# Reassociated matrix products in a four-layer linear-attention and GLU kernel, forward and backward

## The chip, the cores and the metric

The kernel runs on one core of a Trainium2 chip, as one program with one launch. The metric is device time in microseconds (us) from start to end of an execution. The engines are TensorE (PE, with its weight loads PEld), VectorE (DVE), ScalarE (ACT), GpSimd (POOL) and SyncE (SP, which issues DMAs). Each engine takes its instructions from its own queue, in order.

## The reference

Four residual layers share two sets of weights: A (linear attention), B (gated linear unit), A, B. The kernel returns the result and the gradients for the input and for the five weights. Sequence 2048, width 512, 32 heads of 16, inner width 1376, bf16.

```python
def _A_ref(x, wqkv, wo):
    qkv = (x @ wqkv).reshape(B, S, 3, H, Dh).transpose(2, 0, 3, 1, 4)
    q, k, v = qkv[0], qkv[1], qkv[2]
    phi = lambda t: jnp.where(t > 0, t + 1, jnp.exp(t)) + 1e-6
    pq, pk = phi(q), phi(k)
    kv = jnp.einsum("bhsd,bhse->bhde", pk, v)
    z = jnp.einsum("bhsd->bhd", pk)
    num = jnp.einsum("bhqd,bhde->bhqe", pq, kv)
    den = jnp.einsum("bhqd,bhd->bhq", pq, z)[..., None] + 1e-6
    o = num / den
    return o.transpose(0, 2, 1, 3).reshape(B, S, D) @ wo

def _B_ref(x, w_gate, w_up, w_down):
    g = jnp.einsum("bsd,df->bsf", x, w_gate)
    u = jnp.einsum("bsd,df->bsf", x, w_up)
    return jnp.einsum("bsf,fd->bsd", _sigmoid(g) * u, w_down)

x = A_x
x = x + _A_ref(_layernorm(x), A_wqkv, A_wo)
x = x + _B_ref(_layernorm(x), w_gate, w_up, w_down)
x = x + _A_ref(_layernorm(x), A_wqkv, A_wo)
x = x + _B_ref(_layernorm(x), w_gate, w_up, w_down)
# outputs: x, and the gradients for grad_out of A_x, wqkv, wo, w_gate, w_up, w_down
```

## The kernel before, in words

The sequence is cut into 16 row tiles of 128 rows (`st`), the width into 4 chunks of 128 (`NDC`). The residual rows stay in SBUF in float32 (`k.xs`, names `x_93` to `x_108`) and hold the running gradient later. Activations that backward needs go to DRAM in bf16 (`sv_...`). The tile framework orders the instructions of all engines when the program is built: what is written one after another in the code can be interleaved in the queues, so that the matmuls of a weight-gradient stage (`..._p2`) stand between those of a loop that waits for other engines. SP issues nearly all DMAs; only the last stage (names `ta_...`) uses ACT's queue for loads.

`a_fwd` (layers 0 and 2) runs in three stages. For each tile it projects q, k and v (L468, 12 matmuls of 512 columns), forms pq and pk with exp, min and max (L472 to L478), copies v, and transposes pq. Then z = sum of pk (L498, one column each) and kv = pk^T v (L504) over all tiles, masked to the heads' diagonal blocks (`rhsN`). Then, for each tile, num (L521), den (L524), the reciprocal (L528), o = num / den (L530), its transposes, y = o wo (L542), and the add to the residual on POOL (L546). The layer norm of a tile (`FwdLN`) gives h and its transpose hT; the one of the next layer is begun for two tiles (`NPRE`). In both `a_fwd` calls the weights' transposes for backward (`wT_groups`, 52 in all) are interleaved from the fifth tile on.

`b_fwd` (layers 1 and 3) computes the gate, the up product, the transposes and the down product tile by tile.

`a_bwd_p1` has two loops over the tiles. Loop 1: gT (cast on POOL L676, transposes), do = g wo^T (L958), its product with o and the sum over a head (L961, L963), dnA (L966, L968), dkv accumulated over tiles (L973), dnT (L979, L980), dpq (L933, L935), dq (L938) and its transposes. Between the loops the small kv gradients are masked and transposed. Loop 2: transposes of pk and v (L1028), dpk (L1055, L1057), dv (L1061), the transposes of dk and dv, dh = [dq dk dv] wqkv^T (L1038, 12 matmuls), and the layer norm's backward (`ln_bwd_tile`, L646 to L652). `a_bwd_p2` gives the weight gradients from saved rows: dwo = o^T g (L885) and dwqkv = h^T [dq dk dv] (L833). Layer 2's results are kept in DRAM (`dwp_...`), and the later layer's are added to them (L838, `final`).

The order of the backward is b_bwd_p1(3), a_bwd_p1(2), b_bwd_p2(3), b_bwd_p1(1), a_bwd_p2(2), a_bwd_p1(0), b_bwd_p2(1), a_bwd_p2(0).

Of the kernel before, what the change touches and what calls it, by code (L numbers as in the profile page):

```python
# [8 lines left out]
BF16 = mybir.dt.bfloat16  # L9
F32 = mybir.dt.float32  # L10
# [40 lines left out]
def kernel(  # L51
# [18 lines left out]
    phases = "all"  # L70
# [6 lines left out]
    k.phases = phases  # L77
# [44 lines left out]
    for l in range(4):  # L122
# [3 lines left out]
        if l % 2 == 0:  # L126
            for nm in ("pq", "pk", "v", "o"):
                d[nm] = dram.tile([S, D], BF16, name=f"sv_{nm}{l}")
            d["dqkv"] = dram.tile([S, 3 * D], BF16, name=f"sv_dqkv{l}")
# [12 lines left out]
        wqkv=dram.tile([D, 3 * D], BF16, name="dwp_wqkv"),  # L142
        wo=dram.tile([D, D], BF16, name="dwp_wo"),
# [8 lines left out]
    with tc.tile_pool(name="wfwd", bufs=1) as wfwd:  # L152
# [17 lines left out]
        with ExitStack() as lctx:  # L170
# [6 lines left out]
            lns = [FwdLN(k, l) for l in range(4)]  # L177
            if phases != "fwd":
                wtg = wT_groups(k)
                half = 26  # L180
                with tc.tile_pool(name="wt_stage", bufs=2) as wt_stage:
                    a_fwd(k, 0, lns[0], nxt=lns[1],
                          extra=lambda ps_pool: [g(wt_stage, ps_pool) for g in wtg[:half]])
                b_fwd(k, 1, lns[1], nxt=lns[2])
                with tc.tile_pool(name="wt_stage2", bufs=2) as wt_stage:
                    a_fwd(k, 2, lns[2], nxt=lns[3],
                          extra=lambda ps_pool: [g(wt_stage, ps_pool) for g in wtg[half:]])
            else:
                a_fwd(k, 0, lns[0], nxt=lns[1])
                b_fwd(k, 1, lns[1], nxt=lns[2])  # L190
                a_fwd(k, 2, lns[2], nxt=lns[3])
# [9 lines left out]
            b_fwd(k, 3, lns[3], out_cb=out_cb)  # L201

    if phases == "fwd":
        return
# [4 lines left out]
    with ExitStack() as bctx:  # L209
# [13 lines left out]
        def load_a_weights():  # L223
            k.woT = wb.tile([P, NDC, D], BF16, name="woT", tag="w_b")
            nc.sync.dma_start(out=k.woT[:], in_=k.wT["woT"].rearrange("(c p) j -> p c j", p=P))
            k.wqkvT = wb.tile([P, 3 * NDC, D], BF16, name="wqkvT", tag="w_a")
            nc.sync.dma_start(out=k.wqkvT[:], in_=k.wT["wqkvT"].rearrange("(c p) j -> p c j", p=P))
        k.load_b_weights, k.load_a_weights = load_b_weights, load_a_weights
# [7 lines left out]
        o1stg = bctx.enter_context(tc.tile_pool(name="out1_stg", bufs=2))  # L236
        o1cur = {}
# [872 lines left out]
```

## Time and profile before

| | |
|---|---|
| median of 3 runs (lowest, highest) | 1394.34 us (1394.27, 1397.73) |
| span of the profiled execution | 1393.1 us |
| instructions | 25045, of which 9956 matmuls |
| bytes moved by DMA | 269.77 MB, 194 GB/s on the mean |

The times are of whole executions; the profile is one execution, and its span is what its rows add up to. The median is 1.2 us above that span. In a row of the timeline the first number is the start in us from the span's start, the second the length; matmuls are pipelined, so a matmul's length (about 380 ns at 512 columns) is longer than the distance to the next one's start, which is what it costs. The stages in the trace: A-forward of layer 0 from 19.7 to 114.8 us, B-forward 1 to 254.6, A-forward 2 to 346.7, B-forward 3 to 484, b_bwd_p1(3) to 643, loops 1 and 2 of a_bwd_p1(2) to 707 and 787, the rest of b_bwd_p2(3) to 878, b_bwd_p1(1) to 1038, loops 1 and 2 of a_bwd_p1(0) to 1138 and 1217, and the last weight gradients to the end.

### The profile page before, as it was taken

To read this page: it belongs to the slowest core of one execution; us is meant where nothing else is said; L and a number is where in the kernel's file an instruction comes from. 1 tells how busy PE (TensorE), PEld (TensorE's weight loads), DVE (VectorE), ACT (ScalarE), POOL (GpSimd) and SP (SyncE) were. 2 spreads that over 40 slices of the span, in tenths; PEclk is the share of its full clock that TensorE was granted. 3 is DMA by queue.
4 is the path that set the end of the run, shared out by engine and by line. 5 is a ranking of instruction groups with operands and counts; after the bars stand their busy time and mean duration, and the time that the engine had idled before them with its cause. 6 is when DMAs were issued, how large, how long until landed. Compare 5 with 4: busy or idle time off the path is not lost. (4 is left out here: it accounts for less than half of the span.)

```text
span 1393.1 us, 25045 instructions
## 1 busy us (share of the span) xinstructions
PE 1297.9 (93%) x9956; PEld 790.1 (57%) x9956; DVE 679.9 (49%) x1468; ACT 647.3 (46%) x1168; POOL 250.5 (18%) x413
## 2 busy tenths in 40 slices
PE   4989899998899898998999999999999999988988
PEld 2555455556455444554665677555548675556767
DVE  6664644567533355665857400456640676611111
ACT  5857576775776544443547411444431447600000
POOL 4026654105633300002100100010010101100000
PEclk9999999999999999999999999999999999999999
DMA  7622334452543497547774586964568956499745
GB/s 273 230 103 103 149 152 158 147 177 98 201 178 143 169 326 259 175 168 237 218 230 148 181 227 149 334 217 167 172 199 248 275 169 192 143 311 261 175 122 162
DMA packets 268853, 269.77 MB, mean 194 GB/s; under 512 B 24576, under 2 KB 245184, under 8 KB 268736
## 3 DMA queue, kind: packets, MB, share of 16 engines
q1 hardware_dynamic: 246272, 253.50, 57.2%
q10 hardware_dynamic: 22464, 14.68, 3.6%
q8 instruction: 78, 1.28, 0.4%
q14 instruction: 39, 0.32, 0.1%
HBM read 144.57 MB, written 123.57 MB: 192 GB/s over the span
## 5 line engine op out<-in xcount | busy, mean ns | idle before, releaser
L730 ACT COPY ddT<-T_ps 128x1024 bf16<-128x1024 bf16 (+1 forms) x96 | 83.1, 867 | 103.4 <-PE T_ps L728 103.3
L630 POOL TENSOR_TENSOR ssd_t<-hh_t,oms 128x512 bf16<-128x512 bf16 (+1 forms) x96 | 100.6, 1052 | 83.0 <-ACT oms L628 48.4
L648 DVE SCALAR_TENSOR_TENSOR junk<-t_sb,h_ld 128x512 bf16<-128x512 f32 x64 | 46.1, 720 | 137.6 <-ACT t_sb L646 136.6
L762 DVE TENSOR_TENSOR dd_t<-dhh_ps,ssd_ld 128x512 bf16<-128x512 f32 (+1 forms) x96 | 60.4, 629 | 102.0 <-PE dhh_ps L760 102.0
L742 PEld LDWEIGHTS <-ddT 128*128 128x128 bf16 (+1 forms) x704 | 66.3, 98 | 71.4 <-issue 12.5
L468 PE MATMUL mm_ps<-wqkv,hT 128*128 128x512 bf16 x384 | 100.2, 386 | 0.5 <-DVE x_108 L601 0.4
L742 PE MATMUL dh_ps<-wuT,ddT 128*128 128x512 bf16 (+1 forms) x352 | 96.5, 382 | 3.9 <-ACT t_sb L646 0.9
L833 PE MATMUL p_ps<-p_set,p_a_15354 128*128 128x256 bf16 (+1 forms) x768 | 82.5, 267 | 10.8 <-DVE dw_stg L798 10.8
L629 DVE TENSOR_TENSOR hh_t<-u_ps,ssd_t 128x512 bf16<-128x512 f32 (+1 forms) x96 | 60.7, 634 | 65.3 <-PE u_ps L624 50.3
L760 PE MATMUL dhh_ps<-wdT,gT 128*128 128x512 bf16 (+1 forms) x384 | 87.8, 364 | 5.0 <-DMA wdT<-wdT_d 4.3
L624 PE MATMUL u_ps<-wu,hT 128*128 128x512 bf16 (+1 forms) x384 | 92.4, 361 | 0.0
L621 PE MATMUL g_ps<-wg,hT 128*128 128x512 bf16 (+1 forms) x384 | 92.0, 361 | 0.4 <-DVE ostage L530 0.4
L833 PE MATMUL p_ps<-p_set,p_a_10151 128*128 128x256 bf16 (+1 forms) x768 | 81.5, 261 | 0.9 <-DMA p_set<-sv_hdd_130 0.9
L599 PE MATMUL y_ps<-wd,hhT 128*128 128x512 bf16 (+1 forms) x352 | 81.4, 380 | 0.0
L742 PE MATMUL dh_ps<-wgT,ddT 128*128 128x512 bf16 (+1 forms) x352 | 81.3, 379 | 0.0
L833 PEld LDWEIGHTS <-p_a_15354 128*128 128x128 bf16 x768 | 68.9, 100 | 21.7 <-issue 8.4
L590 ACT COPY hhT<-hhT_ps 128x512 bf16<-128x512 bf16 (+1 forms) x96 | 49.5, 515 | 58.3 <-PE hhT_ps L587 58.1
L728 PEld LDWEIGHTS <-dd_t 128*128 128x128 bf16 (+1 forms) x704 | 50.7, 101 | 40.8 <-DVE dd_t L762 18.5
L833 PEld LDWEIGHTS <-p_a_10151 128*128 128x128 bf16 x768 | 67.2, 98 | 9.2
L728 PE MATMUL T_ps<-ident,dd_t 128*128 128x128 bf16 (+1 forms) x704 | 66.4, 221 | 3.6 <-DVE dd_t L762 3.5
L838 DVE TENSOR_TENSOR dw_stg<-p_ps,dw_stg 128x512 bf16<-128x512 f32 (+1 forms) x36 | 23.4, 653 | 87.5 <-PE p_ps L833 74.4
L1038 PE MATMUL dh_ps<-wqkvT,dkvT 128*128 128x512 bf16 x256 | 65.6, 380 | 0.0
(493 smaller groups left out, 2498.3 us busy)
## 6 DMA issues: line engine op xcount, KB each, us to landing
p_set<-sv_hdd_130 SPq DMA_DIRECT2D x15, 1024.0 KB, 7.1
p_set<-sv_hdd_119 SPq DMA_DIRECT2D x15, 1024.0 KB, 6.3
sv_ssd_118<-ssd_t SPq DMA_DIRECT2D x16, 688.0 KB, 3.1
sv_ssd_129<-ssd_t SPq DMA_DIRECT2D x16, 688.0 KB, 3.1
ssd_ld<-sv_ssd_129 SPq DMA_DIRECT2D x16, 688.0 KB, 5.5
sv_hdd_130<-dd_t SPq DMA_DIRECT2D x16, 688.0 KB, 3.9
ssd_ld<-sv_ssd_118 SPq DMA_DIRECT2D x16, 688.0 KB, 6.0
sv_hdd_119<-dd_t SPq DMA_DIRECT2D x16, 688.0 KB, 3.7
```

The lines of the kernel that those rows point to most:

```text
L468: nc.tensor.matmul(ps[:], lhsT=hT[:, kc, :], rhs=k.wqkv[:, kc, n * D:(n + 1) * D], start=(kc == 0), stop=(kc == NDC - 1))
L599: nc.tensor.matmul(y_ps[:], lhsT=T["hhT"][0:r, fc, :], rhs=k.wd[0:r, fc, :], start=(fc == 0), stop=(fc == NFC - 1))
L621: nc.tensor.matmul(g_ps[:, 0:w], lhsT=hT[:, kc, :], rhs=k.wg[:, kc, c0:c0 + w], start=(kc == 0), stop=(kc == NDC - 1))
L624: nc.tensor.matmul(u_ps[:, 0:w], lhsT=hT[:, kc, :], rhs=k.wu[:, kc, c0:c0 + w], start=(kc == 0), stop=(kc == NDC - 1))
L629: nc.vector.tensor_tensor(hh_t[:, c0:c0 + w], u_ps[:, 0:w], ssd_t[:, 0, c0:c0 + w], ALU.mult)
L630: nc.gpsimd.tensor_tensor(ssd_t[:, 1, c0:c0 + w], hh_t[:, c0:c0 + w], oms[:, 0:w], ALU.mult)
L728: nc.tensor.transpose(tps[0:r, a, i, :], dd[:, a, fc * P:fc * P + r], k.ident[:])
L730: nc.scalar.copy(ddT[:, :, fcs[0]:fcs[0] + nfull, :], tps[:, :, 0:nfull, :])
L742: nc.tensor.matmul(dh_ps[:], lhsT=T["ddT"][0:r, a, fc, :], rhs=wT[0:r, fc, :], start=(i == 0), stop=(i == n_mm - 1))
L760: nc.tensor.matmul(dhh_ps[:, 0:w], lhsT=gT[:, jc, :], rhs=k.wdT[:, jc, c0:c0 + w], start=(jc == 0), stop=(jc == NDC - 1))
L833: nc.tensor.matmul(psv[:, icl, :], lhsT=lhs_all[:, st, ic * P:(ic + 1) * P], rhs=set_t[:, st, 0:W], start=(st == 0), stop=(st == NST - 1))
L1038: nc.tensor.matmul(dh_ps[:], lhsT=lhsT, rhs=k.wqkvT[:, n * NDC + c, :], start=(i == 0), stop=(i == 3 * NDC - 1))
```

## The change

Let h be the normed rows, Wv the last third of wqkv, and g the gradient of y. Heads are blocks on the diagonal of a 512x512 matrix, which `bdmask` keeps.

Forward: X = h^T pk is accumulated during the K phase, kv = mask(Wv^T X), M = kv wo, and y = pqn M, where pqn = pq / den, row by row. v and o are never formed. den is the sum over a head of pq z, with z spread over all partitions (`zb`, by a matrix of ones). So `a_fwd` has a K phase (k projection and X), a short chain, and a Q phase (q projection, den, pqn, its transposes; y comes four tiles later, `LA`). The product pq z is on POOL.

Backward, loop 1: dp = g M^T (`MT`, computed forward), c = -sum over a head of dp pqn, and dq = (dp + c z) phi'(q) / den on VectorE and POOL, where phq - EPS, saved forward, is phi'. dz is accumulated (4 matmuls of 8 columns). G = g^T pqn comes behind the loop, kept transposed (`GT`). Then dkv = wo G masked, Nv = Wv dkv and Mv. Loop 2: dpk = h Nv plus dz, dk, and dh = dq Wq^T + pk Mv + dk Wk^T. The gradients of wo and of Wv come at the end from small matrices (`a_small_grads`): kv^T G and X dkv of both layers in one sum.

Moved besides: all 16 tiles' h and hT of an A layer are kept in SBUF (`FwdLNAll`) and hT is saved; layer 2's layer norm is done within `b_fwd` of layer 1; the weights' transposes are now in `b_fwd` 1 (w_gate, w_up, w_down: 34 groups) and `b_fwd` 3 (wqkv, wo: 16 groups). In tiles of loop 1 the loaded phq buffer is overwritten with dq and stored.

```diff
+            for nm in ("hT", "pqn", "phq", "pk"):
                 d[nm] = dram.tile([S, D], BF16, name=f"sv_{nm}{l}")
-            d["dqkv"] = dram.tile([S, 3 * D], BF16, name=f"sv_dqkv{l}")
+            d["dqk"] = dram.tile([S, 2 * D], BF16, name=f"sv_dqk{l}")
...
+            lns = [FwdLNAll(k, l) if l % 2 == 0 else FwdLN(k, l) for l in range(4)]
+            wtg_b, wtg_a = wT_groups(k)
+            a_fwd(k, 0, lns[0], nxt=lns[1])
+            with tc.tile_pool(name="wt_stage", bufs=2) as wt_stage:
+                b_fwd(k, 1, lns[1], nxt=lns[2], extra=wtg_b, wt_stage=wt_stage)
+            a_fwd(k, 2, lns[2], nxt=lns[3])
...
+            woT_GT = wb.tile([P, 2, NDC, D], BF16, name="woT_GT", tag="w_b")
+            k.woT, k.GT = woT_GT[:, 0, :, :], woT_GT[:, 1, :, :]
...
+            MT_X = wb.tile([P, 2, NDC, D], BF16, name="MT_X", tag="w_c")
+            k.MT, k.X_ld = MT_X[:, 0, :, :], MT_X[:, 1, :, :]
+            nc.sync.dma_start(out=k.MT, in_=k.sv[l]["MT"].rearrange("(c p) j -> p c j", p=P))
+            nc.sync.dma_start(out=k.X_ld, in_=k.sv[l]["X"].rearrange("(c p) j -> p c j", p=P))
...
+        a_small_grads(k, RT.big, R.stage, RT.psum)
+        a_bwd_p2(k, RT, 0, True)
...
+                (groups_a if w_sb is k.wqkv or w_sb is k.wo else groups).append(g)
...
+        h_t = self.h_all[:, st, :]
+        layernorm_tile(k, R["small"], k.xs[st], h_t, k.rstd[l][:, st:st + 1])
+        transpose_blocks(k, R["ps"], self.hT_all[:, st, :, :], [h_t[:, c * P:(c + 1) * P] for c in range(NDC)],
...
+LA = 4
...
+        def proj(st, n):
+            ps = ps_kq.tile([P, D], F32, name="mm_ps")
+            for kc in range(NDC):
+                nc.tensor.matmul(ps[:], lhsT=ln.hT_all[:, st, kc, :], rhs=k.wqkv[:, kc, n * D:(n + 1) * D],
+                                 start=(kc == 0), stop=(kc == NDC - 1))
+            return ps
...
+        def phi(ps, a_out, out):
+            e_t = work.tile([P, D], BF16, name="e_t")
+            nc.scalar.activation(e_t[:], ps[:], ACT.Exp)
+            nc.vector.tensor_scalar(a_out, e_t[:], 1.0, EPS, ALU.min, ALU.add)
+            nc.vector.scalar_tensor_tensor(out, ps[:], 1.0 + EPS, a_out, ALU.add, ALU.max)
...
+            def accum_X(st):
+                for ic in range(NDC):
+                    nc.tensor.matmul(X_ps[ic][:], lhsT=ln.h_all[:, st, ic * P:(ic + 1) * P], rhs=pk_all[:, st, :],
+                                     start=(st == 0), stop=(st == NST - 1))
...
+                ps = proj(st, 1)
+                a_t = work.tile([P, D], BF16, name="a_t")
+                phi(ps, a_t[:], pk_all[:, st, :])
...
+        z_ps = ps_kq.tile([P, D], F32, name="mm_ps")
+        for st in range(NST):
+            nc.tensor.matmul(z_ps[:], lhsT=k.ones_sq[:], rhs=pk_all[:, st, :], start=(st == 0), stop=(st == NST - 1))
+        nc.scalar.copy(zb[:], z_ps[:])
...
+            kv_ps = ps_ch.tile([P, NDC, P], F32, name="ch_ps")
             for c in range(NDC):
-                for st in range(NST):
-                    nc.tensor.matmul(z_ps[:, c:c + 1], lhsT=pk_all[:, st, c * P:(c + 1) * P], rhs=k.ones_col[:],
-                                     start=(st == 0), stop=(st == NST - 1))
-            nc.vector.tensor_copy(zcol[:], z_ps[:])
+                cs = slice(c * P, (c + 1) * P)
+                for ic in range(NDC):
+                    nc.tensor.matmul(kv_ps[:, c, :], lhsT=k.wqkv[:, ic, 2 * D + c * P:2 * D + (c + 1) * P],
+                                     rhs=X_sb[:, ic, cs], start=(ic == 0), stop=(ic == NDC - 1))
+            nc.vector.tensor_tensor(kvbdT[:], kv_ps[:], k.bdmask[:].unsqueeze(1).to_broadcast([P, NDC, P]), ALU.mult)
...
+                m_ps = ps_y.tile([P, D], F32, name="y_ps")
+                nc.tensor.matmul(m_ps[:], lhsT=kvbdT[:, c, :], rhs=k.wo[:, c, :], start=True, stop=True)
...
+                ps = proj(st, 0)
+                pq_t = work.tile([P, D], BF16, name="pq_t")
+                phi(ps, cur["phq"][:, st % NB, :], pq_t[:])
+                prod = work.tile([P, D], BF16, name="prod")
+                nc.gpsimd.tensor_tensor(prod[:], pq_t[:], zb[:], ALU.mult)
+                den = small.tile([P, H], F32, name="den")
+                nc.vector.tensor_reduce(den[:], prod[:].rearrange("p (h e) -> p h e", h=H), AX.X, ALU.add)
+                nc.vector.tensor_scalar(den[:], den[:], EPS, None, ALU.add)
+                nc.vector.reciprocal(rden_all[:, st, :], den[:])
+                pqn = cur["pqn"][:, st % NB, :]
+                nc.vector.tensor_tensor(pqn.rearrange("p (h e) -> p h e", h=H),
+                                        pq_t[:].rearrange("p (h e) -> p h e", h=H),
                                         rden_all[:, st, :].unsqueeze(2).to_broadcast([P, H, DH]), ALU.mult)
+                pqnT = stg.tile([P, NDC, P], BF16, name="pqnT", bufs=LA + 1)
...
+            def stage_y(st, pqnT):
                 y_ps = ps_y.tile([P, D], F32, name="y_ps")
                 for c in range(NDC):
-                    nc.tensor.matmul(y_ps[:], lhsT=oT[:, c, :], rhs=k.wo[:, c, :],
+                    nc.tensor.matmul(y_ps[:], lhsT=pqnT[:, c, :], rhs=M_sb[:, c, :],
...
+            Ts = {}
+            for st in range(NST + LA):
+                if st < NST:
+                    Ts[st] = stage_q(st)
+                if st >= LA:
+                    stage_y(st - LA, Ts.pop(st - LA))
...
+                    nc.tensor.matmul(m_ps[:, c * P:(c + 1) * P], lhsT=k.wo[:, c, jc * P:(jc + 1) * P],
+                                     rhs=kvbdT[:, c, :], start=True, stop=True)
...
+            if nxt is not None:
                 nxt.stage(st)
...
+            upto = (st + 1) * len(extra) // NST
+            for g in extra[done:upto]:
+                g(wt_stage, ps_tp2)
+            done = upto
...
+    h_all = p2_load_all(k, R, sv["h"], R.pfx + "_a1")
...
+            for b in range(NST // NB):
+                nc.sync.dma_start(out=pqn_all[:, b * NB:(b + 1) * NB, :], in_=dram_batch(sv["pqn"], b))
+            phld = BatchLoader(k, stg, sv["phq"], "phq_ld", nb=NB2)
...
+                nc.gpsimd.tensor_scalar(g_bf, k.xs[st][:], 1.0, 0.0, ALU.mult, ALU.add)
...
+                ph_st = phld.get(st)
+                pqn_st = pqn_all[:, st, :]
+                dp_ps = ps_mm.tile([P, D], F32, name="dp_ps")
+                for jc in range(NDC):
+                    nc.tensor.matmul(dp_ps[:], lhsT=gT[:, jc, :], rhs=k.MT[:, jc, :],
+                                     start=(jc == 0), stop=(jc == NDC - 1))
+                dp = work.tile([P, D], BF16, name="dp")
+                nc.scalar.copy(dp[:], dp_ps[:])
+                prod = work.tile([P, D], BF16, name="prod", bufs=1)
+                nc.vector.tensor_tensor(prod[:], dp[:], pqn_st, ALU.mult)
+                cneg = small.tile([P, H], F32, name="cneg")
+                nc.vector.tensor_reduce(cneg[:], prod[:].rearrange("p (h e) -> p h e", h=H), AX.X, ALU.add,
+                                        negate=True)
+                cneg_bf = small.tile([P, H], BF16, name="cneg_bf")
...
+                nc.gpsimd.tensor_copy(cneg_bf[:], cneg[:])
...
+                    nc.tensor.matmul(dz_ps[:, c, :], lhsT=pqn_st[:, c * P:(c + 1) * P],
...
+                nc.gpsimd.tensor_tensor(t_t[:].rearrange("p (h e) -> p h e", h=H),
+                                        zb[:].rearrange("p (h e) -> p h e", h=H),
+                                        cneg[:].unsqueeze(2).to_broadcast([P, H, DH]), ALU.mult)
+                nc.vector.scalar_tensor_tensor(ph_st.rearrange("p (h e) -> p h e", h=H),
+                                               ph_st.rearrange("p (h e) -> p h e", h=H), -EPS,
+                                               rden_all[:, st, :].unsqueeze(2).to_broadcast([P, H, DH]),
+                                               ALU.add, ALU.mult)
+                nc.vector.tensor_tensor(t_t[:], dp[:], t_t[:], ALU.add)
+                nc.vector.tensor_tensor(ph_st, t_t[:], ph_st, ALU.mult)
...
+            for jc in range(NDC):
+                ps = ps_mm.tile([P, D], F32, name="dp_ps")
+                for st in range(NST):
+                    nc.tensor.matmul(ps[:], lhsT=g_all[:, st, jc * P:(jc + 1) * P], rhs=pqn_all[:, st, :],
...
+                    nc.tensor.matmul(dkv_ps[:, c, :], lhsT=k.woT[:, jc, cs], rhs=GT[:, jc, cs],
...
+                    nc.tensor.matmul(ps[:, c * P:(c + 1) * P],
+                                     lhsT=k.wqkvT[:, 2 * NDC + c, ic * P:(ic + 1) * P], rhs=dkvbdT[:, c, :],
...
+                nc.tensor.matmul(ps[:], lhsT=dkvbdT[:, c, :], rhs=k.wqkvT[:, 2 * NDC + c, :], start=True, stop=True)
...
+                ops = [(T["pdT"][:, 1, c, :], k.wqkvT[:, c, :]) for c in range(NDC)]
+                ops += [(T["pdT"][:, 0, c, :], Mv[:, c, :]) for c in range(NDC)]
+                ops += [(T["dkT"][:, c, :], k.wqkvT[:, NDC + c, :]) for c in range(NDC)]
...
+                dq_st = dqld.get(st)
+                hT_st = hTld.get(st)
...
+                for a, src in enumerate((pk_st, dq_st)):
+                    for c in range(NDC):
+                        nc.tensor.transpose(tps[:, a, c, :], src[:, c * P:(c + 1) * P], k.ident[:])
+                nc.scalar.copy(pdT[:], tps[:])
...
+                    nc.tensor.matmul(dpk_ps[:], lhsT=hT_st[:, c * P:(c + 1) * P], rhs=Nv[:, c, :],
...
+            a_small_transposes(k, l, big, GT, X_ld, dkvbdT, ps_fin)
...
+def a_small_transposes(k, l, pool, GT, X_ld, dkvbdT, ps_fin):
+    nc = k.nc
+    kvbdT = k.kv[l]["kvbdT"]
+    T = {nm: pool.tile([P, NDC, w], BF16, name=nm) for nm, w in SMALL}
+    jobs = [(T["G"][:, c, :], [GT[:, i, c * P:(c + 1) * P] for i in range(NDC)]) for c in range(NDC)]
+    jobs += [(T["XT"][:, c, :], [X_ld[:, i, c * P:(c + 1) * P] for i in range(NDC)]) for c in range(NDC)]
+    jobs += [(T["kvbd"][:].rearrange("p c f -> p (c f)"), [kvbdT[:, c, :] for c in range(NDC)]),
+             (T["dkvbd"][:].rearrange("p c f -> p (c f)"), [dkvbdT[:, c, :] for c in range(NDC)])]
...
+def a_small_grads(k, pool, stg, psum):
+    nc = k.nc
+    T = {}
+    for l in (2, 0):
+        for nm, w in SMALL:
+            T[nm, l] = pool.tile([P, NDC, w], BF16, name=f"{nm}_ld{l}")
+            nc.sync.dma_start(out=T[nm, l][:], in_=k.sv[l][nm].rearrange("(c p) j -> p c j", p=P))
...
+        for i, l in enumerate((2, 0)):
+            nc.tensor.matmul(ps[:], lhsT=T["kvbd", l][:, c, :], rhs=T["G", l][:, c, :], start=(i == 0), stop=(i == 1))
...
+            for i, l in enumerate((2, 0)):
+                nc.tensor.matmul(ps[:, c * P:(c + 1) * P], lhsT=T["XT", l][:, c, ic * P:(ic + 1) * P],
+                                 rhs=T["dkvbd", l][:, c, :], start=(i == 0), stop=(i == 1))
```

## The prediction

> **What bounds the kernel now.** I read the totals first, then the stretches of the trace by stage, then single instructions. The totals and the groups give the engine:
>
> ```profile
> PE 1297.9 (93%) x9956; PEld 790.1 (57%) x9956; DVE 679.9 (49%) x1468; ACT 647.3 (46%) x1168; POOL 250.5 (18%) x413
> PE 9%; DMA 2%; DVE 0%; SPq 0%; issue 0%; DVEq 0%
> ```
>
> TensorE is busy 93% of the span. The chain that ended last covers only a tenth, so I judge by stage. The stretches of the trace (columns: length, then busy us of PE, PEld, DVE, ACT, POOL, granted clock, DMA share, GB/s) for A-forward of layer 0 (projections; kv and z; then o and y), B-forward of layer 1 and loop 1 of A-backward of layer 2:
>
> ```profile
> 19.70:79.00 59.30, 58.80 (x414) 30.89 (x412) 39.04 (x89) 49.10 (x88) 4.16 (x11) 1.00 0.62 211
> 79.00:88.20 9.20, 7.52 (x134) 7.09 (x134) 4.29 (x16) 1.17 (x2) 0.00 (x0) 0.81 0.51 173
> 88.20:114.80 26.60, 23.69 (x253) 15.02 (x253) 20.06 (x60) 16.32 (x29) 17.14 (x18) 1.00 0.20 67
> 114.80:254.60 139.80, 133.48 (x835) 70.18 (x833) 72.15 (x166) 92.13 (x189) 76.72 (x109) 0.99 0.38 147
> 650.00:707.00 57.00, 52.54 (x507) 35.89 (x507) 49.07 (x125) 28.56 (x49) 7.20 (x12) 1.00 0.78 227
> ```
>
> PE is nearly full everywhere, but in the o/y stretch (20.1 of 26.6) and in loop 1 (49.1 of 57) VectorE follows closely: work moved to it there comes soon to the top. The price of a matmul is read from when the next begins (PE timeline):
>
> ```profile
> 63.36 0.39 PE L318 MATMUL ln_tp<-ident,hstage 128*128 128x128 bf16 x4
> 63.58 0.59 PE L468 MATMUL mm_ps<-wqkv,hT 128*128 128x512 bf16 x2
> ...
> 64.52 2.32 PE L468 MATMUL mm_ps<-wqkv,hT 128*128 128x512 bf16 x10
> 66.67 0.39 PE L318 MATMUL ln_tp<-ident,hstage 128*128 128x128 bf16 x4
> ...
> 799.78 5.51 PE L833 MATMUL p_ps<-p_set,p_a_10151 128*128 128x256 bf16 x49
> 805.13 7.07 PE L863 MATMUL p_ps<-p_a_10156,p_set 128*128 128x512 bf16 x32
> ```
>
> Ten 512-wide ones take 66.67 - 64.52 = 2.15, so 0.215 each; four 128-wide ones 0.22, 0.055 each; 49 256-wide ones 5.35, 0.109 each.
>
> **The change, part by part: PE's work.** Matmuls of one A layer, counted from the loops. Forward: the v projection, pq transposes, kv, num, z (N=1) and den (N=8) over tokens go; X (64 of 512), z by ones (16 of 512), M (4 of 512), kv and MT (16 of 128 each) come: 512-wide +20, 128-wide -168, N=1 -64, N=8 -64. Backward: dnT, dpq, dq's transposes, v's and dv's, dv and dwo go; G (64 of 512), the wide dpk (64 of 512), small products and 40 transposes come; dwqkv loses a third: 512-wide +56, 256-wide -128, 128-wide -316, 136-wide -64, N=8 +64. Both layers: 152 x 0.2155 = +32.8; 256 x 0.109 = -27.9; 968 x 0.0555 = -53.7; 128 of 136 at 0.0585 (scaled) = -7.5; 128 of N=1 at 0.025 (z's 25 begin 0.63 before kv) = -3.2. Sum -59.5 us: -16.4 forward, -43.1 backward. It counts wherever PE remains the bound.
>
> The price of a wide matmul matters here, since wide ones replace narrow ones. The rows say 0.215 and 0.055. The Trainium skill ("TensorE: Matmul & The Clock Gate", section "Back-to-back issue gap") gives about 131 ns at N=512 and 81 ns at N=128 for a sustained stream. By its prices these two shapes would give 152 x 0.131 - 968 x 0.081 = -58.5 instead of -20.9; the trace's 215 and 55 ns decide.
>
> **Forward, the Q phase.** After the K phase (projection and X of 16 tiles: PE 8 x 0.2155 + transposes, about 31 us; ACT's LN, hT and exp rows 0.81 + 0.59 + 0.60 give 32) come about 6 us of X evacuation, z, kv and M, then the Q phase. Per tile PE has only 8 x 0.2155 + 4 x 0.0555 = 1.94. DVE has: min/add on bf16 0.293 (as L984), the max from PSUM 0.685 (L477/L478), reduce 0.675 (L963), den 0.163, reciprocal 0.335 and pqn, a product with a broadcast, 0.68 (L530 reads PSUM, this reads two SBUF inputs): 2.83. POOL has the new product 1.15 (L630's full-width rows) and the x add 1.27 (L546): 2.42. So VectorE becomes the bound. Whether DVE and POOL can run side by side is shown here:
>
> ```profile
> 900.04 0.62 POOL L676 TENSOR_SCALAR gstage<-x_99 128x512 bf16<-128x512 f32 x1 [8.06 <-issue]
> 900.18 1.02 DVE L648 SCALAR_TENSOR_TENSOR junk<-t_sb,h_ld 128x512 bf16<-128x512 f32 x1 [3.33 <-ACT t_sb L646]
> 900.62 1.05 POOL L676 TENSOR_SCALAR gstage<-x_100 128x512 bf16<-128x512 f32 x1
> ```
>
> POOL's cast of 0.62 alone takes 1.05 when it meets DVE's two-input instruction, and that takes 1.02 instead of its usual 0.69: three pieces of 1.93 together took 1.63, between side by side (1.24) and one after another. The Trainium skill ("SBUF — State Buffer", section "Terms") has the port pair of DVE and GpSimd as an exclusive lock held for a whole instruction, the loser fully blocked, which speaks against this change; by it a Q tile would be at least 0.97 + 2.42 = 3.39 and the row's slowdown agrees in kind, not in full.
>
> So a Q tile lies between 2.83 (no conflict) and 3.6 (POOL's 2.42 and DVE's two SBUF-only steps, 0.97, never together, plus hand-overs); I take 3.3, nearer the conflicting row: 53 us, and 4 for the last four y. A-forward 0: 32 + 6 + 57 = 95, as before's 95.1 (19.7 to 114.8). The first projection comes earlier since the LN copies stand ahead of the later x casts: 0 to -5.7, taken -3. Layer 2 has no LN in its K phase: 28 + 6 + 57 = 91 against 92.1. In B-forward 1 the 132 moved weight transposes cost 7.3 and the LN transposes of 14 more tiles 3.1; PE is full there, so +10.4. What they bring to other engines (ACT 14 LN of 0.81 and half of the 34 copies at 0.59, DVE about 1.5 per LN and the other copies, POOL 0.78 per rstd, SP eight stores of 512 KB and the transposed weights') lifts ACT from 92 to about 114 of 150, DVE to 99, POOL to 88: hidden under PE; uncovered it would be ACT's 22. B-forward 3 gets 64 transposes, +3.6. Forward: -3 + 0 - 1 + 10.4 + 3.6 = +10 (its ends by the Q tile: -5 and +20), though PE has 16 less to do.
>
> **Backward, loop 1.** Per tile DVE has the reduce 0.675, the two-input scalar step 0.72 (L648) and three bf16 SBUF products or sums that the trace doesn't show: between 0.293 (one-input bf16) and 0.69 (two inputs, one f32); I take the middle, 0.49, as half lies with each: 2.87. POOL: t_t 1.15, cneg 0.19, g cast 0.617: 1.96. Side by side: 2.87; wholly exclusive 0.72 + 3 x 0.49 + 1.96 = 4.15; I take 3.5: 56 us, and 5 to start (in before gT waited 4.35 for woT). Now PE has 1.2 per tile, 19, and about 18 of filler and neighbouring matmuls in its queue there: it waits 61 - 37 = 24 instead of the 10.5 (layer 2) and 8.4 (layer 0) that these stretches now lie above their issue times. That is +13.5 and +15.6, taken +27 (ends +9 at 2.87, +49 at 4.15). The G products come only behind the last tile, so they can't fill it. The add and product write into the loaded phq buffer, which is stored and then loaded anew: store 4.0 and load 4.5 (rows dqstage, pq_ld) within the 7 of a pair of tiles, two buffers deep: no more than a tie. On SP's queue the 2 MB of pqn go ahead of phq; only the first 512 KB (some 4, as o_ld's 3.8) is awaited, as o_ld was (3.13 at its first prod). The middle chain (dkv, mask, Nv, Mv) replaces the old one: +1, as both are a handful of PSUM hand-overs. In the tail the wait of 4.4 for h, which shares a buffer with o, goes; the three waits on dw_stg (4.5, 2.2, 5.5) stay, bounds ±6. MT and weights asked for earlier: -2. Backward: -43.1 + 27 + 1 - 4.4 - 2 = -21.5.
>
> Sum: +10 - 21.5 = -11.5 on the profiled 1393.1 gives 1381.6; the median of the runs, 1394.34, lies 1.2 above the span, so 1383 us. A difference of 0.3% (4.2 us) is about what a measurement of this kernel tells from none.
>
> **Rivals.** *No conflict*: DVE and POOL run side by side, as the 0.62 beside PSUM readers suggests, and PE's saving comes through: forward -5, backward -43.1 + 9 - 5.4 = -39.5, together -44.5: 1350 us. *The shared port decides (slower)*: every two-input DVE step waits out POOL's, 3.6 per Q tile and 4.15 per tile of loop 1: forward +20, backward -43.1 + 49 - 5.4 = +0.5: 1415 us. For it speaks the 1.02/1.05 pair, against it that the pair cost less than the full sum; it wins over the saving from about 3.6 per tile in loop 1 with 3.5 in Q. *The removed work was not what set the time*: DMA at 78 to 80% in loop 1 and the tail's loads keep the stages as long as now, and only forward moves: 1394 to 1404; against it, PE waits for a DMA in few places.
>
> **How the numbers follow.** Forecast 0.50 (1368 to 1400: about 0.35 faster, 0.09 same, 0.06 slower); no conflict 0.23, all faster; port 0.21 (0.18 slower, 0.03 same); work not the bound 0.06 (0.02 same, 0.04 slower). Together 0.58 faster, 0.14 same, 0.28 slower. The range runs from somewhat under the no-conflict case (three products at 0.4) to the port case: 1343 to 1415.
>
> **What would show it.** Right: 8628 matmuls and PE busy near 1240 us; a Q phase of 50 to 60 us with PE half idle, its waits on DVE's pqn; loop 1 of about 60 with PE waiting for cneg, and POOL's t_t or DVE's products longer than alone; B-forward 1 near 150. Wrong: Q tiles at 2.8 and the bf16 products at 0.3 (then 1350), or t_t and pqn stretched to over 1.5 (then 1415), or waits on phq and MT loads.

## The result, and the profile after

Nine runs of each kernel: 1402.03 us after (1399.38 to 1406.04), 1394.34 before (1391.53 to 1397.73). The ratio is 1.0048 with a 95% interval of 1.0032 to 1.0063: slower, by 0.3% at the least. The profiled execution has a span of 1400.6 us (before 1393.1) and took 1402.44. The forecast was 1383 and faster; the range (1343 to 1415) holds the time, but on the wrong side of the kernel before.

The totals and the engines of the chain that ended last, after:

```profile
PE 1244.4 (89%) x8506; PEld 720.3 (51%) x8628; DVE 712.8 (51%) x1440; ACT 591.1 (42%) x1092; POOL 339.6 (24%) x500
PE 8%; DMA 2%; SPq 1%; DVE 0%; ACT 0%; issue 0%; ACTq 0%; DVEq 0%
```

TensorE's work fell as counted (8628 weight loads, before 9956), yet the span grew. PE's busy time fell from 1297.9 to 1244.4, so by the profile PE idles 156 us instead of 95; but 122 of the matmul records after are missing (8506 of 8628), none before, and at the prediction's prices they are worth up to 26 us, so part of this idle time is only a gap in the record. POOL's busy time rose from 250 to 340. Where PE idles is seen in the stretches after (columns as before: length, busy us of PE, PEld, DVE, ACT, POOL, granted clock, DMA share, GB/s): Q phase and MT of layer 0, B-forward 1, Q phase and MT of layer 2, and a stretch between B-forward 3 and the backward in which PE hardly works:

```profile
57.50:124.90 67.40, 44.06 (x210) 18.50 (x212) 55.81 (x110) 30.28 (x53) 44.37 (x38) 0.85 0.18 63
124.90:276.20 151.30, 144.00 (x965) 76.69 (x982) 81.98 (x192) 102.55 (x206) 71.80 (x104) 0.99 0.47 179
314.00:383.30 69.30, 43.68 (x217) 18.64 (x219) 59.46 (x126) 32.84 (x57) 48.16 (x48) 0.85 0.20 69
521.00:543.00 22.00, 0.84 (x6) 0.48 (x6) 1.12 (x2) 1.82 (x3) 0.00 (x0) 0.58 1.07 349
```

By stages, in us, with the starts taken from the first matmul of each:

| stage | before | forecast | after |
|---|---|---|---|
| to the first projection | 19.7 | 16.7 | 14.0 |
| A-forward 0 | 95.1 | 95 | 110.9 |
| B-forward 1 | 139.8 | 150.2 | 151.3 |
| A-forward 2 | 92.1 | 91 | 107.1 |
| B-forward 3 up to the backward's first dhh (L760, after L795) | 142.8 | 146.4 | 159.5 |
| from there to the end of the span | 903.6 | 882.1 | 857.8 |

The backward saved twice what was forecast, 45.8 us; everything ahead of it took 53.3 more, where 10 were forecast.

**Q phase.** The timeline of POOL and DVE in it shows what holds DVE:

```profile
97.26 1.30 POOL L577 TENSOR_TENSOR x<-y_sb,x 128x512 f32<-128x512 f32 x1
97.29 1.31 DVE L556 TENSOR_SCALAR den<-den 128x32 f32<-128x32 f32 x1
...
98.51 1.16 POOL L553 TENSOR_TENSOR prod<-pq_t,zb 128x512 bf16<-128x512 bf16 x1
98.52 1.31 DVE L491 TENSOR_SCALAR phqstage<-e_t 128x512 bf16<-128x512 bf16 x1
...
102.20 1.27 POOL L577 TENSOR_TENSOR x<-y_sb,x 128x512 f32<-128x512 f32 x1
102.27 0.69 DVE L555 TENSOR_REDUCE den<-prod 128x32 f32<-128x512 bf16 x1 [0.45 <-POOL prod L553]
...
103.89 0.11 DVE L556 TENSOR_SCALAR den<-den 128x32 f32<-128x32 f32 x1
...
104.73 1.46 POOL L553 TENSOR_TENSOR prod<-pq_t,zb 128x512 bf16<-128x512 bf16 x1 [1.26 <-DVE pq_t L492]
105.11 0.34 DVE L557 RECIPROCAL rden_all<-den 128x32 f32<-128x32 f32 x1
```

A step on 32 numbers per row (den, L556), 0.11 us at 103.89, takes 1.31 at 97.29: it began 0.03 after POOL's add and ended 0.04 after it. The same happens to the one-input bf16 step at 98.52, which began 0.01 after POOL's product, ended 0.16 after it and takes 0.28 otherwise. The reduce at 102.27 and the reciprocal at 105.11 ran wholly beside an instruction of POOL and kept their usual length. The groups of DVE in this phase (columns: busy us, mean ns, idle before):

```profile
L559 DVE TENSOR_TENSOR pqnstage<-pq_t,rden_all 128x512 bf16<-128x512 bf16 x16 | 14.3, 895 | 0.0
L555 DVE TENSOR_REDUCE den<-prod 128x32 f32<-128x512 bf16 x16 | 10.9, 681 | 5.5 <-POOL prod L553 5.5
L492 DVE SCALAR_TENSOR_TENSOR pq_t<-mm_ps,phqstage 128x512 bf16<-128x512 f32 x16 | 10.5, 658 | 0.0
L491 DVE TENSOR_SCALAR phqstage<-e_t 128x512 bf16<-128x512 bf16 x15 | 7.8, 521 | 0.0
L556 DVE TENSOR_SCALAR den<-den 128x32 f32<-128x32 f32 x16 | 7.8, 488 | 0.0
L557 DVE RECIPROCAL rden_all<-den 128x32 f32<-128x32 f32 x16 | 5.4, 339 | 0.0
```

The means add to 3.58 us per tile (2.83 was the sum without blocking, 3.3 the value taken), and 5.5 us of waits for POOL's product, 0.34 per tile, come on top.

**The stretch behind B-forward 3.** SP's queue and PE's wait, after:

```profile
522.97 0.67 SPq L207 DMA_DIRECT2D wdT<-wdT_d  x1
523.69 0.90 SPq L211 DMA_DIRECT2D wuT<-wuT_d  x1
524.64 4.68 SPq L213 DMA_DIRECT2D wuT<-wuT_d  x1
529.37 0.65 SPq L211 DMA_DIRECT2D wgT<-wgT_d  x1
530.06 3.63 SPq L213 DMA_DIRECT2D wgT<-wgT_d  x1
533.80 0.37 SPq L701 DMA_DIRECT2D gstage<-in_grad_out_dram  x1
534.22 0.86 SPq L786 DMA_DIRECT2D ssd_ld<-sv_ssd  x1
```

```profile
PE gT_ps L308 <- DMA ssd_ld<-sv_ssd: 20.4, 1, 20.4
```

The first rows of grad_out and ssd stand behind 4 MB of weights and are issued at 533.8; PE waits 20.4 us. Before, the first of these loads was issued at 350.4, during B-forward 3, as its tile's row shows:

```profile
L666 SPq DMA_DIRECT2D gstage<-in_grad_out_dram x8: 373/384/462, 350.4 to 591.3; - x8
```

### The profile page after: what moved, and what is told of

The parts are those of the page before. It is cut to its first block, busy times and chain, and to the rows that moved or that the text cites. A ratio compares the mean times of both kernels' runs of the same rounds, so it can differ in the third digit from the quotient of the medians.

```text
span 1400.6 us, 22220 instructions
## 1 busy us (share of the span) xinstructions
PE 1244.4 (89%) x8506; PEld 720.3 (51%) x8628; DVE 712.8 (51%) x1440; ACT 591.1 (42%) x1092; POOL 339.6 (24%) x500
## 5 line engine op out<-in xcount | busy, mean ns | idle before, releaser
L868 PE MATMUL p_ps<-p_set,p_a 128*128 128x256 bf16 (+1 forms) x1792 | 194.6, 267 | 10.5 <-DVE dw_stg L873 7.4
L868 PEld LDWEIGHTS <-p_a 128*128 128x128 bf16 x1792 | 161.3, 99 | 33.6 <-issue 6.5
L661 POOL TENSOR_TENSOR ssd_t<-hh_t,oms 128x512 bf16<-128x512 bf16 (+1 forms) x96 | 101.7, 1062 | 99.6 <-ACT oms L659 60.1
L683 DVE SCALAR_TENSOR_TENSOR junk<-t_sb,h_ld 128x512 bf16<-128x512 f32 x64 | 45.8, 715 | 139.8 <-ACT t_sb L681 139.7
L685 POOL TENSOR_SCALAR ab<-c 128x2 f32<-128x2 f32 x64 | 12.2, 191 | 384.2 <-DVE junk L683 373.9
L777 PEld LDWEIGHTS <-ddT 128*128 128x128 bf16 (+1 forms) x704 | 65.9, 97 | 68.9 <-issue 10.4
L681 ACT ACTIVATE t_sb<-dh_ps,rstd_all 128x512 f32<-128x512 f32 x64 | 44.0, 687 | 133.0 <-issue 60.4
L795 PE MATMUL dhh_ps<-wdT,gT 128*128 128x512 bf16 x383 | 87.2, 364 | 2.8 <-ACT gT L317 2.8
L484 PE MATMUL mm_ps<-wqkv,hT_all 128*128 128x512 bf16 x249 | 73.0, 409 | 14.2 <-DVE pq_t L492 13.9
L898 PE MATMUL p_ps<-p_a,p_set 128*128 128x512 bf16 (+1 forms) x331 | 79.0, 379 | 2.5 <-DMA p_set<-sv_hdd 2.0
L629 PE MATMUL y_ps<-wd,hhT 128*128 128x512 bf16 (+1 forms) x336 | 78.3, 379 | 1.2 <-DVE x L631 0.4
L553 POOL TENSOR_TENSOR prod<-pq_t,zb 128x512 bf16<-128x512 bf16 x32 | 43.3, 1357 | 93.5 <-DVE pq_t L492 90.1
```

Of the source, the lines that this page charges most:

```text
L484: nc.tensor.matmul(ps[:], lhsT=ln.hT_all[:, st, kc, :], rhs=k.wqkv[:, kc, n * D:(n + 1) * D], start=(kc == 0), stop=(kc == NDC - 1))
L629: nc.tensor.matmul(y_ps[:], lhsT=T["hhT"][0:r, fc, :], rhs=k.wd[0:r, fc, :], start=(fc == 0), stop=(fc == NFC - 1))
L661: nc.gpsimd.tensor_tensor(ssd_t[:, 1, c0:c0 + w], hh_t[:, c0:c0 + w], oms[:, 0:w], ALU.mult)
L777: nc.tensor.matmul(dh_ps[:], lhsT=T["ddT"][0:r, a, fc, :], rhs=wT[0:r, fc, :], start=(i == 0), stop=(i == n_mm - 1))
L795: nc.tensor.matmul(dhh_ps[:, 0:w], lhsT=gT[:, jc, :], rhs=k.wdT[:, jc, c0:c0 + w], start=(jc == 0), stop=(jc == NDC - 1))
L868: nc.tensor.matmul(psv[:, icl, :], lhsT=lhs_all[:, st, ic * P:(ic + 1) * P], rhs=set_t[:, st, 0:W], start=(st == 0), stop=(st == NST - 1))
```

## Experiments

The theories: (1) DVE, blocked by POOL, sets the Q phases' length; (2) the wait behind B-forward 3 comes from the SBUF that the change keeps occupied; (3) B-forward 1 grows by what was moved into it. Rivals: a lower granted clock (0.85 in the Q phases), the weights' transfers by themselves, PE's issue. Stage times below are from each run's profile; the changed kernel's are in the table above.

**e1, e7, e9: the wait.** e1 moves all weight transposes (50 groups by the code, not 52) to B-forward 1:

```diff
-                b_fwd(k, 1, lns[1], nxt=lns[2], extra=wtg_b, wt_stage=wt_stage)
+                b_fwd(k, 1, lns[1], nxt=lns[2], extra=wtg_b + wtg_a, wt_stage=wt_stage)
...
-            with tc.tile_pool(name="wt_stage2", bufs=2) as wt_stage:
-                b_fwd(k, 3, lns[3], out_cb=out_cb, extra=wtg_a, wt_stage=wt_stage)
+            b_fwd(k, 3, lns[3], out_cb=out_cb)
```

> All 50 groups of weight transposes stand in B-forward 1, none in B-forward 3. Buffer theory (the first loads of the backward wait for a staging buffer that the transposes in B-forward 3 hold to its end): PE's gap of 20.6 us behind B-forward 3 shrinks to about 5, as before had 4.5; B-forward 1 grows by 3.6 and B-forward 3 shrinks by as much; total 1402 -> about 1386. Rival (4 MB of weights fill the DMA engines there in any order): the gap stays above 15 us and the total within 3 us of 1402.

Measured: 1403.93, ratio 1.0063 (1.0042 to 1.0085). B-forward 1 takes 156.6; g's first load is still issued only at 532.7. This is what the rival, the weights' transfers, had said would come. e7 leaves the transposes where they were and instead gives back h_all and hT_all (`...` stands for the calls up to `a_fwd(k, 2, ...)`, now inside that block):

```diff
-            k.hres = lctx.enter_context(tc.tile_pool(name="ln_hall", bufs=1))
+            with tc.tile_pool(name="ln_hall", bufs=1) as hres:
+                k.hres = hres
...
```

> The buffers h_all and hT_all (32 KB of each partition) are given back behind A-forward 2 instead of at the end of the forward; the weight transposes stay in B-forward 3 as in the changed kernel. Residency theory (moving the transposes' staging alone left the gap, so it is h_all that pushes the backward's first stage buffers onto memory of B-forward 3): the loads of g and of ssd are issued during B-forward 3, as in before, the gap of 20.6 us falls to about 5 and the total to about 1386. Rival (the weights wdT, wuT, wgT, asked for at the same place, are what lands last): the gap stays over 12 us, total 1398 or more.

Measured: 1400.60, ratio 1.0056 (1.0040 to 1.0072); g's first load at 532.5. ssd's loads now stand early in the queue (the first at 403.0), but g's do not. This expectation was missed too. e9 has both edits and no other:

> Against the changed kernel only the memory: h_all and hT_all given back behind A-forward 2, and all weight transposes (with their staging) in B-forward 1, so that B-forward 3 holds neither. Each alone left the gap. Overlap theory (either of the two lies over the buffers of g, so both must go): the gap behind B-forward 3 falls from 20.6 to about 6, B-forward 1 grows by 4 to 5, B-forward 3 shrinks by 4, total 1402 -> 1384. Rival (in the run with three edits it was the shorter forward that helped, not memory): gap over 15 and total 1400.

Measured: 1390.69, ratio 0.9969 (0.9955 to 0.9984). The tile's row and PE's waits at that place (500 to 532 us):

```profile
L701 SPq DMA_DIRECT2D gstage<-in_grad_out_dram x8: 372/384/1147, 394.0 to 629.0; - x8
```

```profile
PE dhh_ps L795 <- DMA wdT<-wdT_d: 4.3, 1, 4.3
PE gT_ps L308 <- ACT gT L317: 1.4, 2, 0.7
```

g is loaded at 394, and what is left is the 4.3 us for wdT that before had as well (4.33). B-forward 3 up to the first dhh takes 141.2 instead of 159.5: 18.3 back, of which the 64 transposes are 3.6. B-forward 1 pays 5.3 for them. So either buffer alone held the loads back, and both had to go. That the loads' tiles lie in the memory of these two buffers is inferred from the three runs; no view shows addresses. With this wait gone the changed kernel is 0.3% faster than before.

**e2, e3: the Q phase.** e2 puts the product on DVE, e3 the residual's add as well:

```diff
-                nc.gpsimd.tensor_tensor(prod[:], pq_t[:], zb[:], ALU.mult)
+                nc.vector.tensor_tensor(prod[:], pq_t[:], zb[:], ALU.mult)
```

and in e3 also

```diff
-                y_sb = work.tile([P, D], F32, name="y_sb")
-                nc.scalar.copy(y_sb[:], y_ps[:])
-                nc.gpsimd.tensor_tensor(k.xs[st][:], y_sb[:], k.xs[st][:], ALU.add)
+                nc.vector.tensor_tensor(k.xs[st][:], y_ps[:], k.xs[st][:], ALU.add)
```

> The product pq z of the Q phase moves from POOL to DVE; nothing else. Port theory (POOL's instructions block DVE's two-input and bf16 scalar steps): DVE gains a product of about 0.42 (L964 unblocked) but den falls from 0.49 to 0.2, min/add from 0.52 to 0.35, pqn from 0.90 to 0.75, and the 5.5 us of waits for POOL's product go: each Q phase 67 -> 60 to 63, total 1402 -> 1388 to 1394. Rival (it is DVE's own work that bounds, blocking or not): 32 x 0.42 = 13 us more, 1415.

> In the Q phases both POOL steps go: the product is on DVE, and the residual's add too, straight from y's PSUM (ACT's copy of y goes). Port theory: with POOL silent, DVE's steps fall to their lengths alone: min/add 0.28, den 0.12, pqn 0.67, product 0.42; DVE then has 3.85 per tile and the Q phases stay at 66 to 70 as in the run with the product alone on DVE: total 1390 to 1396. Rival (hand-overs between engines, not blocking, stretched them): the steps keep 0.35, 0.4, 0.73 and 0.54, and the phases grow by the add's 11 us each.

Measured: e2 1392.42, ratio 0.9977 (0.9957 to 0.9998); e3 1393.94, ratio 1.0006 (0.9995 to 1.0016). From the end of X to B-forward 1, layers 0 and 2: 73.6 and 75.5 us in the changed kernel, 69.8 and 71.4 in e2, 70.0 and 70.5 in e3. DVE was given more to do and the stage became shorter. The groups of e3:

```profile
L559 DVE TENSOR_TENSOR pqnstage<-pq_t,rden_all 128x512 bf16<-128x512 bf16 x16 | 10.9, 681 | 0.0
...
L553 DVE TENSOR_TENSOR prod<-pq_t,zb 128x512 bf16<-128x512 bf16 x16 | 6.3, 392 | 0.0
...
L491 DVE TENSOR_SCALAR phqstage<-e_t 128x512 bf16<-128x512 bf16 x15 | 4.3, 286 | 0.0
L556 DVE TENSOR_SCALAR den<-den 128x32 f32<-128x32 f32 x16 | 2.8, 175 | 0.0
```

With POOL silent pqn falls from 895 to 681 ns, min/add from 521 to 286 and den from 488 to 175; with the add alone on POOL (e2) they are 731, 350 and 417. The difference between the changed kernel and e3, 0.76 us per tile in these three steps, is the blocking, shown by taking POOL away. The reduce and the reciprocal (681 and 339 in the changed kernel, 680 and 346 in e3) do not move.

**e5: the clock.** Four 512-wide matmuls, overwritten by the next, ahead of each y:

```diff
+                for c in range(NDC):
+                    nc.tensor.matmul(y_ps[:], lhsT=k.ident[:], rhs=M_sb[:, c, :], start=True, stop=True)
```

> Four 512-wide matmuls, overwritten by the next, are added ahead of each y in the Q phases (128 in all, 0.86 us per tile): PE then has 2.8 of a tile's 3.6 to 4. Clock theory (the granted clock of 0.85 there, from an idle PE, lengthens the Q phase): the clock returns to near 1 and each Q phase is 5 us or more shorter. Port theory: the Q phases keep 67 and 69 within 2 us whatever the clock, total within 4 us of 1402. PE-bound: 13.8 us more in each, 1430.

Measured: 1404.02, ratio 1.0071 (1.0049 to 1.0093). The stretch of the Q phase in layer 0, which had a clock of 0.85:

```profile
57.50:125.00 67.50, 49.97 (x272) 22.43 (x275) 53.42 (x110) 30.07 (x53) 44.57 (x38) 0.97 0.18 63
```

The clock is back at 0.97 and 13.8 us of matmuls are added, and the phase keeps its 67.4. Neither the clock nor PE's issue sets it in layer 0; layer 2's stage is 2.9 longer.

**e6: loop 1.** c z on DVE in place of POOL (`nc.gpsimd` to `nc.vector` for t_t):

> c z of loop 1 (t_t) moves from POOL to DVE; nothing else. Balanced theory: DVE gains 0.68 per tile (as pqn alone), loses 0.3 of blocking and its waits for t_t (6 us in layer 2): each loop within 3 us of now, total within 6 us of 1402. Rival (POOL's blocking bounds loop 1 as it does the Q phase): each loop 1 is 5 us or more shorter, total 1392 or less.

Measured: 1407.34, ratio 1.0084 (1.0052 to 1.0116); loop 1 with G 62.3 and 60.2 us (61.9 and 57.8). There is no gain: the product costs DVE 0.70 us per tile, and what goes in return is 0.35 of blocking in its other steps (791 to 682 ns in L978, 586 to 412 in L983, 485 to 422 in L964) and 0.38 of waits for POOL's t_t (6.0 us in layer 2), about as much.

**e4, e8, e12: the transposes in the Q phases.** The groups are called from within the Q loop; all their copies go to ACT, and their staging has one buffer in layer 0:

```diff
                 if st < NST:
                     Ts[st] = stage_q(st)
+                    for g in extra[st * len(extra) // NST:(st + 1) * len(extra) // NST]:
+                        g(wt_stage, ps_ch)
```

> The 50 groups of weight transposes stand in the Q phases (34 in layer 0, 16 in layer 2), all their copies on ACT; MT takes X's buffer. If the Q phases are held by DVE and POOL alone, PE and ACT have room there: Q phases the same within 3 us, B-forward 1 shorter by 8 to 11, B-forward 3 by 3 to 4; the gap behind B-forward 3 stays: total 1402 -> 1389. Rival (the Q phase is a chain through ACT's copies of pqnT and y, so that ACT's 20 us more lengthen it): Q phase 0 longer by 10 or more, total unchanged.

Measured: 1406.93, ratio 1.0103 (1.0086 to 1.0119), a miss: layer 0's chain, Q phase and MT take 84.2 instead of 73.6, where PE waits 8.6 us for the copies to the staging buffer and ACT 5.0 for its stores; and B-forward 1 still takes 149.3, with 132 transposes less (7.3 us at 0.0555). e8 has these, e2's edit and the freed buffers:

> Product on DVE, h buffers given back behind A-forward 2, weight transposes in the Q phases. If the three causes are separate, their gains add: -10, -15, -12: 1402 -> 1365. If the gap closes only partly or the Q phases fill up with ACT, 1375 to 1385.

Measured: 1376.03, ratio 0.9881 (0.9866 to 0.9896). The stage of layer 0 is 70.2, as in e2, with the 34 groups in it; B-forward 1 stays at 149.8. Why the same groups cost 10.6 us in e4 and nothing here was not taken apart; PE's wait for their copies is 4.0 here instead of 8.6. e12 is e8 with the transposes in B-forward 1 (e9 and e2 together):

> As the run with both buffers freed, and the product of the Q phase on DVE: transposes in B-forward 1. If the two causes add, 10 less than that run: about 1374. If the transposes in the Q phases were a gain of their own in the run with three edits, this one is above its 1376 by 5 or more; if B-forward 1 has another bound than PE (it kept 149.8 there with 10 us less of matmuls), this one lies 5 to 8 above as well, from its 156; about the same if not.

Measured: 1382.73, ratio 0.9910 (0.9881 to 0.9939): 8.0 below e9, so the gains add, and 6.7 above e8, nearly all in B-forward 1 (157.3).

**e10, e14: the moved layer norm.** In B-forward 1 only two tiles of layer 2's norm are done, as before:

```diff
-            if nxt is not None:
+            if nxt is not None and st < NPRE:
                 nxt.stage(st)
```

> The run with three edits, and the layer norm of layer 2 is done in A-forward 2's K phase for 14 of 16 tiles, instead of within B-forward 1. Theory (in B-forward 1 the second layer norm's chain DVE, POOL, DVE, ACT stands before PE's transposes, two waits of 0.6 per tile, not PE's matmuls): B-forward 1 149.8 -> 136 to 140, K phase of layer 2 35.2 -> 39 to 41 as in layer 0; total 1376 -> 1368 to 1372. PE-bound theory, as predicted: B-forward 1 only 3 shorter, K phase 3 longer: total unchanged.

Measured on e8: 1365.81, ratio 0.9789 (0.9771 to 0.9807), 10.2 below e8. B-forward 1 in e8 and in e10:

```profile
121.80:271.60 149.80, 131.64 (x818) 68.45 (x834) 74.06 (x172) 92.08 (x188) 70.82 (x102) 0.99 0.39 149
```

```profile
121.70:258.80 137.10, 130.15 (x790) 66.24 (x790) 69.05 (x160) 90.70 (x188) 71.05 (x102) 0.96 0.39 150
```

PE is busy for 1.5 us less and the stage is 12.7 shorter; the K phase grows by 0.4. In e8's waits PE's transposes (ln_tp, in order in its queue) stand for ACT's norm:

```profile
PE ln_tp L309 <- ACT hstage L301: 8.4, 13, 0.7
PE ln_tp L309 <- ACT h_all L301: 8.1, 14, 0.8
```

These are two chains per tile, 16.5 us in all; in e10 both are nearly gone (0.6 and 1.1). The same edit on the changed kernel alone:

> The changed kernel with one edit: layer 2's layer norm back in its own K phase for 14 of 16 tiles. Tells the moved layer norm's price apart from the moved transposes' (both stand in B-forward 1, predicted together at 10.4 us as matmuls that PE must issue). Chain theory: B-forward 1 151 -> 141 to 144, K phase of layer 2 31.6 -> 36 to 38, total 1402 -> 1396 to 1398. Issue theory (only the 3.1 us of transposes move): B-forward 1 148, K phase 35, total unchanged within 2.

Measured: 1400.14, ratio 1.0040 (1.0023 to 1.0057). B-forward 1 takes 145.6 instead of 151.3, the K phase of layer 2 33.0 instead of 31.6: between the two theories. PE's wait for h_all is 5.8 us in the changed kernel and 0.7 in e14; that it is smaller than in e8 because the weights' transposes in the same queue cover part of it was not tested.

**e11, e13: q in the K phase.** Projection and phi of q stand in the K phase, kept in SBUF; pqn overwrites it. e11 has this on top of e8; e13 has it on top of e12, with the layer norm of layer 2 in its K phase. Both also cut y_sb from three buffers to two (in e13 no wait of ACT for POOL's add shows):

```diff
+                phi(proj(st, 0), phqst[:, st % NB, :], pq_all[:, st, :])
...
-                ps = proj(st, 0)
-                pq_t = work.tile([P, D], BF16, name="pq_t")
-                phi(ps, cur["phq"][:, st % NB, :], pq_t[:])
+                pq_t = pq_all[:, st, :]
```

> The run with three edits, and the q projection and phi(q) stand in the K phase (kept in SBUF; pqn overwrites them). DVE theory (the Q phase is as long as DVE's work with POOL's blocking, the K phase has DVE room): DVE in Q falls from 3.4 to about 2.4 per tile, Q phases 64 -> 42 to 46; K phases grow by PE's 0.86 to 1.3 per tile, 37 -> 52 and 35 -> 49; total 1376 -> 1366. Rival (the y chain or POOL's add at 1.4 per tile holds the Q phase): Q phases stay over 52 and the total rises to 1380 or more.

> Q projection and phi(q) in the K phase, product on DVE, both buffers freed, layer 2's norm in its K phase, weight transposes in B-forward 1: the Q phases hold no transposes, whose staging waited for its stores in the run before (7.7 us) and whose copies shared one PSUM buffer. If they held that Q phase at 73, both Q phases fall to 45 to 52 with the chain, K phases are 47 to 50, B-forward 1 145 to 148; total 1357 to 1366. Rival (y and POOL's add hold it): Q phases stay at 57 or more, total 1372 or more.

Measured: e11 1388.91, ratio 0.9954 (0.9939 to 0.9970); e13 1381.94, ratio 0.9904 (0.9883 to 0.9926). Both missed. The K phases are no longer than expected (47.9, and 46 to 47), but the chain and Q phase without transposes (e13) still take 59.5 and 60.1. DVE in e13's Q phase:

```profile
L559 DVE TENSOR_TENSOR pq_all<-pq_all,rden_all 128x512 bf16<-128x512 bf16 x16 | 15.5, 977 | 0.0
L555 DVE TENSOR_REDUCE den<-prod 128x32 f32<-128x512 bf16 x15 | 9.6, 640 | 0.0
L553 DVE TENSOR_TENSOR prod<-pq_all,zb 128x512 bf16<-128x512 bf16 x14 | 6.9, 495 | 0.0
L556 DVE TENSOR_SCALAR den<-den 128x32 f32<-128x32 f32 x16 | 6.8, 432 | 0.0
```

With the reciprocal's 0.338 that is 2.88 per tile, where the steps alone have 2.27 (e3's means): with less to do DVE met POOL's add more often, pqn at 977 instead of 681 (731 in e2, which also has only the add on POOL). 16 tiles make 46 us; the rest is the chain, layer norm tiles and the last y. What was moved cost the K phases 10 to 14 us each (37.5 and 31.6 in e12, which does not have the norm of layer 2 in its K phase) and gave the Q phases back 10 to 14 (69.2 and 74.0 in e12, with the chain and MT).

## Why the prediction went wrong

**Right.** PE's saving: 1328 matmuls less. By the weight loads, of which none is missing, and the prediction's prices, issue time fell by 60 us (59.5 forecast). The first projection came 5.7 us earlier, the far end of 0 to -5.7. B-forward 1 at 151.3 was forecast at 150.2. VectorE did become the bound of the Q phases, and the mechanism of the slower rival, POOL's steps blocking DVE's, is what e2 and e3 show there, though it does not decide loop 1 (e6). The prices of the unseen bf16 products were near: L964 0.485, L982 0.446, L983 0.586, taken 0.49.

**Wrong: "I take 3.3", the Q tile.** It measured 3.58 of DVE time plus 0.34 of waits for POOL's product, 3.9, beyond even the bound of 3.6. The steps counted as blocked were too few: only pqn and min/add, 0.97, were put against POOL, but den, a step on 32 columns with one f32 input, waits whole instructions as well. And the layer norm tiles that share DVE there, 3.9 us in layer 0, had no term. The phases took 67.4 and 69.3, MT's 3 in it, where 57 was summed: 22.7 us of the miss, some 20 of it the tile's 3.9 instead of 3.3 (0.6 over 32 tiles). Whether blocking is full was the choice of the sum. "Not in full" was read from one pair, and even that pair says little for it: DVE's 1.02 ends 0.54 after POOL's first cast, and the second cast ends 0.47 after DVE's, where alone they take 0.69 and 0.62, so most of each ran after the other. The rows of the blocked steps now agree with the Trainium skill ("SBUF — State Buffer", section "Terms"), in which the loser blocks for the whole instruction: 1.31 against POOL's 1.30.

**Wrong: no term for the loads behind B-forward 3.** The sum named the stores of the moved transposes on SP's queue, but had no term for where their staging and the kept h lie: by e1, e7 and e9, SBUF that the backward's first loads had been using early. This stretch took 16.7 us more, and e9 gives 18.3 back. The order of SP's queue in the trace shows it: g's first load stands 44 places ahead of wdT's before, and 5 behind it after.

**Wrong: the K phases,** 37.3 and 31.6 instead of 32 and 28: 9 us. The sum let PE and ACT overlap without a loss. PE's issue times there are 31.9 and 29.1, so 5.4 and 2.5 are waits and gaps, for which there was no term; no run took them apart.

**Wrong in the other direction: the backward,** -45.8 (with the gap not in it) against -21.5. PE's issue time fell as forecast there (42.8 by the weight loads, 43.1 forecast); what failed is the waits, +21.6 in the forecast and about -3 measured. "It waits 61 - 37 = 24": loop 1 with G lies 17.0 and 13.2 above its issue times, against 10.5 and 8.4 before, so about 11 more instead of 27. A tile there has about 3.0 us of DVE (3.5 taken), and the forecast left G's 13.8 behind a full 61, where the two together take 61.9 and 57.8. Loop 2 had no term for its waits: it lies less than 0.5 above its issue times, before 6.8 and 5.3, about 11 us less. The 4.4 us in the tail did not show: the tail lies 27.1 above its issue times, before 26.8. The wait for h is gone there, but new ones came, 2.0 for p_set and 3.0 for the copies of the small gradients.

**B-forward 1: the size was right and the reason only in part.** Its 10.4 were costed as PE's matmuls. By the weight loads its issue time grew by only 6.0, partly because 12 matmuls of A-forward 0's last y had run in it before; the other 5.5 are waits and gaps. e14 gives back 5.7 for taking out the layer norm, whose matmuls are 3.1 at most, and e10 12.7: the waits for the norm's chain in PE's queue had no term. That the sum still came out near 11.5 is luck.

So PE's 59.5 came through where it was the bound, in the backward. In the forward it was paid back and more: A-forwards longer by 15.8 and 15.0 us, B-forward 1 by 11.5, the turn to the backward by 16.7, against 5.7 gained at the start. The time lies within the range because two errors offset each other, 43 us too little ahead of the backward and 24 too much in it. With the Q phase's product on DVE, the two buffers freed, the transposes in the Q phase and the norm in its K phase (e10) the reassociated kernel takes 1365.81, 0.979 of before.

## What to carry to other kernels

Work taken off a 93% busy engine is worth its time only where the next engine is not already close: look up the second engine in each stage, and price steps of two engines that block each other as a sum, not as a maximum: here POOL's 2.42 and the three blocked steps of DVE, 1.14 alone, make 3.6 per tile, where 2.83 was DVE's work and 3.9 was measured. Buffers kept alive longer are a cost in time where later loads are to lie in the same memory; look at where the first loads of the next phase stand in their queue. When several causes hold one wait, undoing one of them shows nothing; undo both before the theory is dropped.

## What the runs showed of the hardware

POOL blocks not only DVE's wide two-input steps: a one-input step on 128x32 f32 took 1.31 us in place of 0.11, beside POOL's add of 1.30, while a reduce (681 ns with and without POOL) and a reciprocal (339) ran beside it. The same step pqn, with POOL's add alone beside it, took 731 ns in the mean in e2 and 977 in e13, where DVE has less to do; 681 without POOL. A lower granted clock in a stage where PE waits anyway cost nothing in layer 0: raising it from 0.85 to 0.97 left 67.4 us at 67.5.
